# Two-bank feed-forward units that share PSUM tiles with the scores, q and k in one tile, and a new order of steps

## The chip, the cores and the metric

The kernel runs on one core of one Trainium2 chip. Times are device microseconds (us) of that core; lower is better. The five engines that matter here each work through a list of their own in program order: PE (TensorE, matrix products), DVE (VectorE), ACT (ScalarE), POOL (GpSimd) and SP, which issues every DMA. They meet only through semaphores, so an instruction at the head of a list that waits for another engine holds up all that stands behind it on its own.

## The reference

Eight sequences of 448 tokens, twelve heads of 64, model width 768. First an attention with capped scores, then a gated feed-forward layer with a causal convolution of five taps:

```python
scores = cap * np.tanh(q @ k.T / 8 / cap)          # cap = 30
attn   = np.exp(scores - max) / sum                # over the keys
x      = attn @ v                                  # heads side by side: 448 x 768
gate   = sigmoid(sum_i conv_w[i] * shift(x, 4 - i))
out    = (gate * (x @ w_val)) @ w_out
```

w_val, w_out and conv_w come as float64 and are turned into float32 parts by the kernel.

## The kernel before, in words

**Tiling.** Two heads make a pair of 128 rows; there are 48 pairs p, six to a sequence (batch) b. Scores are computed transposed: one `scores(p, i)` (line 317) fills 112 keys by 448 queries for both heads, in two PSUM banks, with the two heads on the two halves of the array's rows. From pair 13 on (NPLAIN) q and k are split into a high and a low float32r part (`half_hi`, `half_lo`, lines 307 and 312), and a score is three products, high-high, high-low, low-high; before that it is one float32 product. ACT then does `tanh` (330) and `exp` (335) in place of two banks each; DVE adds up the exponentials (`add`, 339); PE makes attention times v (`av`, 355) and the sums of exponentials (`sums`, 366), both as float32 products with the two heads on the two halves of the array's columns. DVE turns the sums, takes the reciprocal and multiplies (`turn_sums`, `recip`, `spread`, `mul`: 378 to 404). `x_hi` (ACT) and `x_lo` (DVE) split the result; `conv` makes the gate, its first tap on ACT for p < 11.

**Feed-forward.** For each batch and each of six column blocks d, `val` (438) adds 18 products (six input blocks c, three float32r products each) in one bank; `gate` (DVE, 450) multiplies by the sigmoid; `gated_hi` (ACT) and `gated_lo` (DVE) split that. `out_part` (466) makes one tile of 128 tokens by 384 columns in one bank from 18 products, six or eight tiles a batch; `store` (479) copies it out of PSUM on ACT and `store_out` issues its DMA. `val` and `out_part` are each cut in two halves that are placed separately.

**PSUM.** Eight banks: two score tiles of two banks (`ps_s`), one bank each for `av` and `sums` (`ps_a`), two single banks for the feed-forward (`ps_f`, lent to `av` and `sums` for odd p below 6).

**Order.** The engines' lists are written out by hand. Each step has a time in units of one pair, in the tables at lines 41 to 114 (STEADY, EARLY, TOGETHER, VAL, OUT_EVEN, W_AT and others); `at` collects (time, step), and the steps are emitted in the sorted order with automatic scheduling off for all engines. So a number in a table is a place in every queue that the step uses, SP's included. The three loads of a pair are four DMAs for q, four for k and two for v; a weight block comes in twice, as `w_raw` and, shifted by two bytes, as `w_late`, and is split by `weight_first` (ACT), `weight_second` and `weight_third` (DVE). There is one buffer each of `w_raw` and `w_late`, two of q, k and v.

**Activation sets.** All six sigmoids of a batch stand together at 7.44 (6.92 in the first batch), between pairs' tanh and exp.

Of the kernel before, what the change touches and what calls it, by code (L numbers as in the profile page):

```python
# [35 lines left out]
NX = 7  # L36
NXX = 8
NPT = 6


STEADY = {
    "load_q": -1.9,
    "load_k": -1.85,
    "load_v": -0.6,
    "tq": -0.90,
    "tk": -0.85,
    "scores": (0.0, 0.05, 0.62, 0.67),
    "tanh": (0.06, 0.13, 0.68, 0.75),
    "exp": (0.22, 0.29, 0.82, 0.89),
    "add": (0.52, 1.03, 1.06),  # L50
    "av": (1.10, 1.15, 1.20, 1.25),
    "sums": (1.28,),
    "turn_sums": 1.41,
    "recip": 1.42,
    "spread": 1.44,
    "mul": 1.50,
    "x_hi": 1.52,
    "x_lo": 1.58,
    "conv": (1.60, 1.61, 1.64, 1.67, 1.70),
}  # L60

SPLIT = STEADY | {"q_hi": -0.69, "k_hi": -0.68, "q_lo": -0.475, "k_lo": -0.47}
PAIRED = STEADY | {"add": (0.52, 1.03), "sums": (1.28, 1.29)}
EARLY = {
    "load_q": -1.9,
    "load_k": -1.85,
    "load_v": -0.7,
    "tq": -0.72,
    "tk": -0.70,
    "scores": (-0.50, -0.49, 0.10, 0.11),  # L70
    "tanh": (0.0, 0.01, 0.35, 0.36),
    "exp": (0.17, 0.18, 0.52, 0.53),
    "av": (0.28, 0.37, 0.65, 0.80),
    "sums": (0.29, 0.38, 0.66, 0.81),
    "turn_sums": 1.02,
    "recip": 1.03,
    "spread": 1.04,
    "mul": 1.05,
    "x_hi": 1.30,
    "x_lo": 1.34,  # L80
    "conv": (1.31, 1.50, 1.52, 1.54, 1.56),
}

SIXTH = PAIRED | {k: EARLY[k] for k in ("tq", "tk", "scores", "tanh", "exp")} | {"add": (0.38, 0.62)}


TOGETHER = {
    "scores": (0.0, 0.05, 0.31, 0.32),
    "tanh": (0.06, 0.13, 0.34, 0.36),
    "exp": (0.22, 0.29, 0.47, 0.53),  # L90
    "add": (0.52, 0.60, 0.61),
}
NEXT_TOGETHER = {
    "turn_sums": 1.41, "recip": 1.42, "spread": 1.43, "mul": 1.44, "x_hi": 1.45, "x_lo": 1.54,
    "conv": (1.58, 2.16, 2.17, 2.18, 2.19),
}
PREPARE_TOGETHER = {"q_hi": -0.69, "k_hi": -0.68, "q_lo": -0.44, "k_lo": -0.43}

LATE_X = {"x_lo": 1.76, "conv": (1.78, 1.80, 1.83, 1.86, 1.89)}
NEARLY, NPAIRED, NPLAIN = 6, 11, 13  # L100

VAL_FIRST = (6.50, 6.85, 7.36, 7.74, 8.36, 8.74)
VAL = (6.85, 7.36, 7.74, 8.36, 8.74, 9.36)
SIG_FIRST, SIG_AT = 6.92, 7.44
OUT_EVEN = (9.80, 10.36, 10.74, 11.36, 11.74, 12.36)
OUT_ODD = (9.80, 10.36, 10.74, 10.80, 11.36, 11.74, 11.80, 12.36)
OUT_LATE = (9.80, 10.36, 10.74, 11.74, 12.36, 12.60)
PART = 0.13
KEEP_AT = 10.2
W_AT = (0.70, 1.70, 2.70, 3.70, 4.70, 5.70, 7.1, 8.0, 8.9, 9.7, 10.4, 11.0)  # L110
W_LOAD = -0.5
W_SECOND, W_THIRD, W_THIRD_EARLY = 0.02, 0.05, 0.71
W_FREE = 11.3
CW_LOAD, CW_AT = -0.55, 0.6
EPS = 1e-9
# [13 lines left out]
def float64_split(nc, raw, mid, hi, lo, t):  # L129
# [16 lines left out]
    def third():  # L146
# [7 lines left out]
def load_conv_w(nc, pool, conv_w, cw):  # L154
# [13 lines left out]
    def make():  # L168
        halves = raw.bitcast(U16).rearrange("p n (k h) -> p n k h", h=1)[:, :, 1:3, 0]
        nc.gpsimd.tensor_copy(mid.bitcast(U16).rearrange("p (n k) -> p n k", k=2), halves)  # L170
        for step in float64_split(nc, raw, mid, cwf, lo, t):
            step()
        nc.vector.tensor_tensor(cwf, cwf, lo, op=ALU.add)
# [27 lines left out]
def fast_path(tc, io, u2, q, k, v, w_val, conv_w, w_out, out, capt):  # L201
# [22 lines left out]
    with ExitStack() as ctx:  # L224
        cpool = ctx.enter_context(tc.tile_pool(name="cpool", bufs=1))
        wk = ctx.enter_context(tc.tile_pool(name="wk", bufs=2))
        ps_s = ctx.enter_context(tc.tile_pool(name="ps_s", bufs=2, space=PSUM))
        ps_a = ctx.enter_context(tc.tile_pool(name="ps_a", bufs=1, space=PSUM))
        ps_f = ctx.enter_context(tc.tile_pool(name="ps_f", bufs=2, space=PSUM))
# [4 lines left out]
        def free_scratch():  # L234
            scratch.pop("w").close()
            scratch["qk"] = ctx.enter_context(tc.tile_pool(name="halves", bufs=2))
# [25 lines left out]
        wstate = {}  # L262
# [11 lines left out]
        def late_load(n):  # L274
# [5 lines left out]
            wstate[n] = wstate[n], shifted(late, NH)  # L280

        def weight_first(n):
            _, c, nh, w = wsteps[n]
            t = wsc.tile([P, WC, NH], I32, name="w_t")
            wstate[n] = float64_split(nc, *wstate[n], w[:, c, nh, 0], w[:, c, nh, 1], t)
# [5 lines left out]
        def weight_third(n):  # L291
            wstate.pop(n)[2]()

        state = {}
        loads, vloads = {(name, 0): t[:, PAD:] for name, t in zip("qk", u2)}, {}

        def load(name, src, p):
            if p:
                loads[name, p] = io.tile([P, S], F32, name=name + "n")
                load_blocks(nc, loads[name, p], src, p)  # L300

        def turn(name, p):
            t = wk.tile([P, S], F32, name=name + "t")
            nc.vector.transpose(t, loads.pop((name, p)))
            state.setdefault(p, {})[name] = t

        def half_hi(name, p):
            st = state[p]
            st[name, "h"] = scratch["qk"].tile([P, S], F32R, name=name + "h")
            nc.scalar.copy(st[name, "h"], st[name])  # L310

        def half_lo(name, p):
            st = state[p]
            st[name, "l"] = scratch["qk"].tile([P, S], F32R, name=name + "l")
            less(nc.vector, st[name, "l"], st.pop(name), st[name, "h"])

        def scores(p, i):

            st = state[p]
            ps = ps_s.tile([P, 2, 512], F32, name="pss")  # L320
            c = slice(i * CH, (i + 1) * CH)
            parts = [("k", "q")] if p < NPLAIN else [(("k", x), ("q", y)) for x, y in ("hh", "hl", "lh")]
            for n, (x, y) in enumerate(parts):
                for j, r in enumerate(ROWS):
                    nc.tensor.matmul(  # L325
                        ps[:CH, j, :S], st[x][r, c], st[y][r], start=(n == 0), stop=(n == len(parts) - 1)
# [3 lines left out]
        def tanh(p, i):  # L330
            st = state[p]
            st["p", i] = wk.tile([CH, 2, S], F32, name="pt", bufs=NPT)
# [16 lines left out]
        def bank(p, name):  # L349

            if p < NEARLY and p % 2:
                return ps_f.tile([P, 512], F32, name="psf")
# [13 lines left out]
        def sums(p, i):  # L366

            st = state[p]
            n = len(tables[p]["sums"])
# [5 lines left out]
            if i == n - 1:  # L375
                vloads.pop(p)
# [20 lines left out]
        xs = {}  # L397
        gates = {}

        def norm_mul(p):  # L400
# [3 lines left out]
            gates[p] = wk.tile([P, S], F32, name="gate", bufs=NX), u  # L404

        def x_hi(p):
            xh = wk.tile([P, S], F32R, name="xh", bufs=NXX)
            nc.scalar.copy(xh, gates[p][1][:, PAD:PAD + S])  # L408
            xs[p] = xh

        def x_lo(p):
            xl = wk.tile([P, S], F32R, name="xl", bufs=NXX)
            less(nc.vector, xl, gates[p][1][:, PAD:PAD + S], xs[p])
            xs[p] = xs[p], xl

        def conv(p, i):
            hp = p % NPAIR
            g, u = gates[p]
# [6 lines left out]
            if i == KW - 1:  # L425
                gates[p] = g

        def sigmoid(b, d):
            g = gates[b * NPAIR + d]
# [307 lines left out]
```

## Time and profile before

| | before |
|---|---|
| median of 3 runs | 754.07 us (752.65 to 757.52) |
| profiled execution: span from first to last instruction, the only time given of it | 750.1 us |
| mean granted TensorE clock | 0.996 |
| busy: PE / DVE / ACT / POOL | 724.0 / 591.8 / 533.8 / 7.6 us |
| share of the span: PE / DVE / ACT | 97% / 79% / 71% |
| instructions | 10863 |
| first matmul starts, last matmul starts | 7.70 us, 744.33 us |
| moved by DMA | 63.75 MB |

A row of a group gives the line, the engine, the operation, output and inputs, the shape, the count, the busy time, the mean length of one, and the idle time of the engine just ahead of the group with what ended it. A row of the timeline gives start, length, engine and instruction. The recorded length of a matmul runs on into the next one, so the time that a matmul takes up in a stream is read from the starts of two neighbours.

### The profile page before, as it was taken

What the parts mean: (1) busy time and instruction counts of PE and PEld (TensorE: products, weight loads), DVE (VectorE), ACT (ScalarE), POOL (GpSimd) and SP (SyncE); (2) the same over time, 40 slices, a digit from 0 to 9 for tenths busy, and PEclk for the clock granted to TensorE, in tenths of its full rate; (3) what the DMA queues carried; (4) which work ended last, traced back from release to release, by engine and by line L of the source; (5) the groups of instructions that cost most, each with busy time, mean ns of one, the idle gap of its engine ahead of it and who ended that gap; (6) DMA issues with size and microseconds to landing.
All of it is one profiled execution on the core that took longest, in us unless ns stands there. A gap on an engine that the chain in (4) does not pass through costs nothing.

```text
span 750.1 us, 10863 instructions
## 1 busy us (share of the span) xinstructions
PE 724.0 (97%) x3972; PEld 487.7 (65%) x3972; DVE 591.8 (79%) x972; ACT 533.8 (71%) x708; POOL 7.6 (1%) x16
## 2 busy tenths in 40 slices
PE   5999998999899999999999999999999999999997
PEld 2333654556667777577576866767766776666996
DVE  2799988987987689888898769988898778988410
ACT  4899967777857678686967579487786768775311
POOL 0000000000000000000000000000000000000000
PEclk9999999999999999999999999999999999999999
DMA  6978766753223242234231333223322233200001
GB/s 108 230 191 219 204 168 146 195 131 77 48 38 80 70 84 38 49 71 86 48 67 42 78 81 63 49 63 77 73 38 60 69 79 64 50 24 32 22 21 67
DMA packets 241820, 63.75 MB, mean 85 GB/s; under 512 B 228448, under 2 KB 235616, under 8 KB 241760
## 3 DMA queue, kind: packets, MB, share of 16 engines
q1 hardware_dynamic: 241760, 62.98, 37.4%
q8 instruction: 33, 0.54, 0.3%
q14 instruction: 27, 0.22, 0.1%
HBM read 51.94 MB, written 11.01 MB: 84 GB/s over the span
## 4 chain that ended last, share of the span: by engine, by line
PE 50%; DVE 18%; ACT 16%; issue 3%; SPq 1%; DMA 0%; DVEq 0%; ACTq 0%
PE pss L325 9%; PE psf L474 7%; PE psf L476 7%; PE psf L475 7%; PE psa L362 6%; ACT pt L333 5%; DVE gate L424 5%; PE psf L445 4%; PE psf L446 4%; PE psf L447 4%; ACT pt L337 3%; DVE pa L347 3%; PE psz L374 3%; ACT gate L430 3%; DVE pa L344 2%
## 5 line engine op out<-in xcount | busy, mean ns | idle before, releaser
L333 ACT ACTIVATE pt<-pss,rc 112x896 f32<-112x896 f32 x192 | 185.4, 1006 | 38.9 <-PE pss L325 38.9
L337 ACT ACTIVATE pt<-pt,capt 112x896 f32<-112x896 f32 x192 | 189.7, 1042 | 0.1
L362 PE MATMUL psa<-pt,vn 112*64 112x448 f32 x720 | 146.9, 546 | 0.0
L424 DVE SCALAR_TENSOR_TENSOR gate<-u,cw,gate 128x448 f32<-128x448 f32 x192 | 131.6, 685 | 5.2
L474 PE MATMUL psf<-wo,g_h 128*128 128x384 f32 x336 | 116.6, 347 | 1.2 <-ACT g_h L454 1.2
L476 PE MATMUL psf<-wo,g_l 128*128 128x384 f32 x336 | 113.3, 337 | 0.2
L475 PE MATMUL psf<-wo,g_h 128*128 128x384 f32 x336 | 112.4, 334 | 0.0
L445 PE MATMUL psf<-xh,wv 128*128 128x448 f32 x288 | 107.5, 373 | 2.1 <-DVE gate L451 2.0
L447 PE MATMUL psf<-xl,wv 128*128 128x448 f32 x288 | 104.4, 363 | 0.0
L446 PE MATMUL psf<-xh,wv 128*128 128x448 f32 x288 | 104.3, 362 | 0.0
L362 PEld LDWEIGHTS psa<-pt,vn 112*64 112x64 f32 x720 | 47.4, 136 | 81.1 <-issue 68.1
L347 DVE TENSOR_TENSOR pa<-pt 112x896 f32<-112x896 f32 x84 | 91.0, 1084 | 11.4 <-ACT pt L337 11.4
L474 PEld LDWEIGHTS psf<-wo,g_h 128*128 128x128 f32 x336 | 63.0, 188 | 16.7 <-issue 12.5
L482 ACT COPY osb<-psf 128x384 f32<-128x384 f32 x56 | 26.7, 478 | 61.6 <-PE psf L476 59.9
L454 ACT CAST g_h<-gate 128x448 fp32r<-128x448 f32 x48 | 26.3, 563 | 61.6 <-DVE gate L451 61.5
L382 DVE STREAM_TRANSPOSE zt<-psz 128x448 f32<-128x448 f32 x45 | 28.8, 641 | 52.0 <-PE psz L374 51.9
L445 PEld LDWEIGHTS psf<-xh,wv 128*128 128x128 f32 x288 | 54.0, 187 | 22.1 <-issue 5.4
L476 PEld LDWEIGHTS psf<-wo,g_l 128*128 128x128 f32 x336 | 63.0, 188 | 2.2 <-DVE g_l L239 2.2
L475 PEld LDWEIGHTS psf<-wo,g_h 128*128 128x128 f32 x336 | 63.1, 188 | 0.0
L325 PE MATMUL pss<-qt,kt 64*112 64x448 f32 x208 | 51.2, 610 | 10.0 <-DVE guard L248 7.7
L325 PE MATMUL pss<-qh,kh 64*112 64x448 f32 x280 | 58.5, 412 | 0.0
L408 ACT CAST xh<-u 128x448 fp32r<-128x448 f32 x48 | 27.2, 568 | 42.4 <-DVE u L403 42.2
(74 smaller groups left out, 905.5 us busy)
## 6 DMA issues: line engine op xcount, KB each, us to landing
vn<-in_v_dram SPq DMA_DIRECT2D x96, 112.0 KB, 2.6
out_dram<-osb SPq DMA_DIRECT2D x56, 192.0 KB, 1.9
qn<-in_q_dram SPq DMA_DIRECT2D x188, 56.0 KB, 2.5
kn<-in_k_dram SPq DMA_DIRECT2D x188, 56.0 KB, 2.5
w_raw<-in_moe_w_val_dram SPq DMA_DIRECT2D x12, 384.0 KB, 5.4
w_late<-in_moe_w_val_dram SPq DMA_DIRECT2D x12, 384.0 KB, 4.2
w_raw<-in_moe_w_out_dram SPq DMA_DIRECT2D x12, 384.0 KB, 3.8
w_late<-in_moe_w_out_dram SPq DMA_DIRECT2D x12, 384.0 KB, 4.3
```

The costliest lines, as they stand in the source:

```text
L325: nc.tensor.matmul(ps[:CH, j, :S], st[x][r, c], st[y][r], start=(n == 0), stop=(n == len(parts) - 1))
L333: nc.scalar.activation(st["p", i], st.pop(("s", i)), AF.Tanh, scale=rc8[:CH])
L337: nc.scalar.activation(t, t, AF.Exp, scale=capt[:CH])
L347: nc.vector.tensor_tensor(st["a", i], st["p", 2 * i], st["p", 2 * i + 1], op=ALU.add)
L362: nc.tensor.matmul(st["o"][r, :S], vloads[p][:, j, i], t[:, j], start=(i == 0), stop=(i == NKT - 1))
L424: nc.vector.scalar_tensor_tensor(g, u[:, i:i + S], cw[:, hp, i:i + 1], g, ALU.mult, ALU.add)
L445: nc.tensor.matmul(o, w_h, xh, start=(c == 0), stop=False)
L446: nc.tensor.matmul(o, w_l, xh, start=False, stop=False)
L447: nc.tensor.matmul(o, w_h, xl, start=False, stop=(c == NCC - 1))
L474: nc.tensor.matmul(o, g_h[:, d, s], w_h, start=(d == 0), stop=False)
L475: nc.tensor.matmul(o, g_h[:, d, s], w_l, start=False, stop=False)
L476: nc.tensor.matmul(o, g_l[:, d, s], w_h, start=False, stop=(d == NCC - 1))
```

## The change

1. `ps_f` is gone. `ps_s` has three tiles of two banks, and scores, `val`, `out_tile` and (odd p below 6) `av` with `sums` take them in turn.
2. `val(b, e)` does two column blocks at once, 36 products in a two-bank tile; `out_tile(b, t)` does 128 tokens by all 768 columns, 36 products. Neither is cut into halves. The number and kind of products is the same.
3. `gate`, `sigmoid`, `gated_hi`, `gated_lo` and `store` work on 896 (store: 768) columns at once, so there are half as many of them. `osb` has one buffer of double size, and a store is one DMA of double size.
4. q and k stand in one tile: `turn`, `half_hi` and `half_lo` are one instruction instead of two (pair 0 keeps two transposes).
5. The tables are replaced by PAIR, BATCH and WEIGHTS, one number for every step and every one of 29 columns (pairs 0 to 14, a cycle of 12 pairs, the last two); `load_v`, weight loads and stores have new places too. In the repeating part the four scores of a pair stand together, ahead of a `val` or `out_tile` or behind one, and sigmoids stand at two places (even batches) or three (odd ones).
6. The space of the weights' scratch tiles, free once the weights are split, gives more buffers late in the run (`late`): the high part of q and k, one more of `gate` and of `x`, two more of `pt`.

```diff
-        ps_s = ctx.enter_context(tc.tile_pool(name="ps_s", bufs=2, space=PSUM))
+        ps_s = ctx.enter_context(tc.tile_pool(name="ps_s", bufs=3, space=PSUM))
         ps_a = ctx.enter_context(tc.tile_pool(name="ps_a", bufs=1, space=PSUM))
-        ps_f = ctx.enter_context(tc.tile_pool(name="ps_f", bufs=2, space=PSUM))
+
+        def banks():
+            return ps_s.tile([P, 2, 512], F32, name="pss")
...
+        def turn(p):
+            t = wk.tile([P, 2, S], F32, name="qkt")
+            if p:
+                nc.vector.transpose(t.rearrange("p j s -> p (j s)"), loads.pop(p).rearrange("p j s -> p (j s)"))
...
+        def half_hi(p):
+            st = state[p]
+            st["h"] = scratch["late"].tile([P, 2, S], F32R, name="qkh")
+            nc.scalar.copy(st["h"], st["l"])
...
+        def sigmoid(b, e):
+            g = pairs[b * NPAIR // 2 + e]
             nc.scalar.activation(g, g, AF.Sigmoid)
...
+        def val(b, e):
+            psums[b, e] = o = banks()
+            for c in range(NCC):
                 xh, xl = xs[b * NPAIR + c]
-                w_h, w_l = (wv[:, c, d // NPH, x, cols] for x in range(2))
-                nc.tensor.matmul(o, w_h, xh, start=(c == 0), stop=False)
-                nc.tensor.matmul(o, w_l, xh, start=False, stop=False)
-                nc.tensor.matmul(o, w_h, xl, start=False, stop=(c == NCC - 1))
+                for j in range(2):
+                    d = 2 * e + j
+                    cols = slice(d % NPH * P, (d % NPH + 1) * P)
+                    w_h, w_l = (wv[:, c, d // NPH, x, cols] for x in range(2))
+                    nc.tensor.matmul(o[:, j, :S], w_h, xh, start=(c == 0), stop=False)
+                    nc.tensor.matmul(o[:, j, :S], w_l, xh, start=False, stop=False)
+                    nc.tensor.matmul(o[:, j, :S], w_h, xl, start=False, stop=(c == NCC - 1))
...
+        def out_tile(b, t):
+            t0 = TL * (1 - b % 2) + t * P
+            s = slice(t0, t0 + P)
+            psums[b, "o", t] = o = banks()
             g_h, g_l = gated["h"], gated["l"]
+            for d in range(NCC):
+                for nh in range(2):
+                    w_h, w_l = (wo[:, d, nh, x] for x in range(2))
+                    nc.tensor.matmul(o[:, nh, :NH], g_h[:, d, s], w_h, start=(d == 0), stop=False)
...
+        def store(b, t):
             row = b * S - TL * (b % 2) + t * P
+            osb = wk.tile([P, 2, NH], F32, name="osb", bufs=1)
+            nc.scalar.copy(osb, psums.pop((b, "o", t))[:, :, :NH])
```

Of the tables, the rows that the prediction speaks of (the columns are batch 0, batch 1, the even ones, the odd ones and the last):

```diff
+BATCH = {
+    "sigmoid": (
+        (6.8378, 7.1151, 7.3249, 5.4748, 6.5827),
+        (7.0106, 8.7084, 6.8322, 8.4311, 7.4049),
+        (7.6515, 9.8857, 7.5925, 9.522, 9.3631),
+    ),
+    "val": (
+        (6.992, 7.5079, 7.2616, 7.6082, 7.6597),
+        (7.6034, 8.623, 8.4304, 8.6508, 7.68),
+        (8.8352, 9.6391, 9.3585, 9.6306, 9.4801),
+    ),
...
+    "out_tile": (
+        (11.3777, 10.6175, 10.1157, 10.6972, 10.6774),
+        (11.9328, 11.3228, 11.1432, 11.3339, 11.5725),
+        (12.5653, 12.1816, 12.3996, 12.1317, 11.8472),
+        (None, 13.1921, None, 13.0834, 12.6071),
+    ),
...
+WEIGHTS = {
+    "weight_load": (-4.3624, .9119, 2.3733, 3.1736, 4.1326, 4.9596, 6.5272, 7.0111, 8.1881, 9.2169, 9.598, 10.6669),
```

In the lists that the new tables give, the steps at the start come in these orders. SP: v of pair 0, `w_raw` 0, q of pair 1, k of pair 1, `w_late` 0, q and k of pair 2, conv_w, v of pair 1. PE: scores 0 and 1 of pair 0, its scores 3, `av` 0, its scores 2, then scores 0 of pair 1. In the repeating part (batch 3): val(3,2), two scores of pair 28, three `av` and the `sums` of pair 27, its last `av`, two scores of pair 28, out_tile(3,0).

More of the change, by code (lines that the diff above doesn't have):

```diff
@@ L34 @@
 WC = 2
-NX = 7
 NXX = 8
 NPT = 6
[L41 to L59, printed above, removed]
-}
@@ L62 @@
[L62 to L81, printed above, removed]
-}
@@ L84 @@
[L84 to L91, printed above, removed]
-}
[L93 to L97, printed above, removed]
@@ L170, in make @@
         nc.gpsimd.tensor_copy(mid.bitcast(U16).rearrange("p (n k) -> p n k", k=2), halves)
-        for step in float64_split(nc, raw, mid, cwf, lo, t):
-            step()
+        first, second, third = float64_split(nc, raw, cwf, lo, t)
+        first()
+        second()
+        third(mid)
         nc.vector.tensor_tensor(cwf, cwf, lo, op=ALU.add)
@@ L368, in sums @@
             st = state[p]
-            n = len(tables[p]["sums"])
+            n = sum(row[column(p)] is not None for row in PAIR["sums"])
             if i == 0:
@@ L395, in spread, with gate_of @@
             nc.vector.transpose(st["zt"].rearrange("p (c e) -> p c e", e=BLK), rc)
-        xs = {}
-        gates = {}
+        xs, us, pairs = {}, {}, {}
+        def gate_of(p):
+            e = p // 2
+            if e not in pairs:
+                late = p >= NLATE and e % (NG + 1) == NLATE // 2 % (NG + 1)
+                pairs[e] = (scratch["late"] if late else wk).tile([P, 2, S], F32, name="gate", bufs=1 if late else NG)
+            return pairs[e][:, p % 2]
         def norm_mul(p):
@@ L459, in keep_tail, with gate, gated_hi, gated_lo @@
+        def gate(b, e):
+            g = pairs[b * NPAIR // 2 + e]
+            nc.vector.tensor_tensor(g, psums.pop((b, e))[:, :, :S], g, op=ALU.mult)
+        def gated_hi(b, e):
+            nc.scalar.copy(gated["h"][:, 2 * e:2 * e + 2, TL:], pairs[b * NPAIR // 2 + e])
+        def gated_lo(b, e):
+            r = slice(2 * e, 2 * e + 2)
+            less(nc.vector, gated["l"][:, r, TL:], pairs.pop(b * NPAIR // 2 + e), gated["h"][:, r, TL:])
         def keep_tail():
@@ new lines, in fast_path @@
+        steps = dict(
+            sigmoid=sigmoid, val=val, gate=gate, gated_hi=gated_hi, gated_lo=gated_lo, out_tile=out_tile, store=store, store_out=store_out,
+        )
+        for name, f in steps.items():
+            for i, row in enumerate(BATCH[name]):
+                for b in range(B):
+                    if row[batch_column(b)] is not None:
+                        at(NPAIR * b + row[batch_column(b)], f, b, i)
+        for b in range(0, B, 2):
+            at(NPAIR * b + BATCH["keep_tail"][0][batch_column(b)], keep_tail)
```

395 lines of the change are left out of this document (253 added, 142 removed).

## The prediction

> **What bounds the kernel now.** I read the page's busy shares, then the windows over one repeating stretch, then the timeline for what a matmul takes up, and last the rows in which PE waits.
>
> ```profile
> span 750.1 us, 10863 instructions
> ...
> PE 724.0 (97%) x3972; PEld 487.7 (65%) x3972; DVE 591.8 (79%) x972; ACT 533.8 (71%) x708; POOL 7.6 (1%) x16
> ```
>
> PE is the bound, but its recorded matmuls overlap, so 97% does not say how much could go. The repeating unit is two batches, 12 pairs. From the sigmoids of batch 2 (277.29 us) to those of batch 4 (452.28):
>
> ```profile
> 277.29:361.48 84.19, 83.60 (x482) 58.02 (x481) 74.16 (x121) 64.31 (x86) 1.73 (x2) 1.00 0.32 64
> 361.48:452.28 90.80, 90.15 (x518) 64.36 (x517) 73.79 (x121) 65.28 (x88) 0.00 (x0) 1.00 0.31 64
> 277.29:452.28 174.99, 173.75 (x998) 122.39 (x997) 147.95 (x241) 129.59 (x174) 1.73 (x2) 1.00 0.31 64
> ```
>
> (Columns: length, then busy of PE, weight loads, DVE, ACT, POOL, clock, DMA share.) The clock is full. How much of 174.99 is products, seen from the starts:
>
> ```profile
> 238.29 0.33 PE L474 MATMUL psf<-wo,g_h 128*128 128x384 f32 x1
> ...
> 238.81 0.33 PE L474 MATMUL psf<-wo,g_h 128*128 128x384 f32 x1
> ...
> 240.19 0.34 PE L476 MATMUL psf<-wo,g_l 128*128 128x384 f32 x1
> 240.46 0.46 PE L325 MATMUL pss<-qh,kh 64*112 64x448 f32 x2
> 240.76 0.37 PE L325 MATMUL pss<-ql,kh 64*112 64x448 f32 x2
> 240.96 0.36 PE L325 MATMUL pss<-qh,kl 64*112 64x448 f32 x2
> 241.16 0.36 PE L325 MATMUL pss<-qh,kh 64*112 64x448 f32 x2
> ...
> 241.56 0.37 PE L325 MATMUL pss<-qh,kl 64*112 64x448 f32 x2
> 241.86 1.35 PE L362 MATMUL psa<-pt,vn 112*64 112x448 f32 x6
> ```
>
> ```profile
> 158.88 1.69 PE pss L325 x8
> ...
> 241.93 3.16 PE psa L362 x16
> ```
>
> ```profile
> 186.10 0.36 PE L445 MATMUL psf<-xh,wv 128*128 128x448 f32 x1
> ...
> 186.70 0.36 PE L445 MATMUL psf<-xh,wv 128*128 128x448 f32 x1
> ...
> 188.50 0.38 PE L325 MATMUL pss<-qh,kl 64*112 64x448 f32 x2
> ...
> 190.87 0.47 PE L445 MATMUL psf<-xh,wv 128*128 128x448 f32 x1 [1.99 <-DVE gate L451]
> ...
> 191.18 0.36 PE L446 MATMUL psf<-xh,wv 128*128 128x448 f32 x1
> 191.38 0.37 PE L447 MATMUL psf<-xl,wv 128*128 128x448 f32 x1
> ```
>
> Three output products take 0.52 us (238.29 to 238.81), three value products 0.60, two score products side by side 0.20, four `av` steps 3.16 in the chain (and two float32 score steps, before pair 13, 1.69). By the code, 12 pairs hold 216 value products (43.2 us), 252 output products (43.7), 48 score steps of three (28.8), 48 `av` and 12 `sums` steps of 0.79 (47.4): 163.1 us. The other 11.9 are two things.
>
> First, **switches** between products that fill the array and products on half of it. 240.19 to 240.46 is 0.27 where 0.17 is usual; the first score product of a burst holds the next up for 0.30 instead of 0.20, and so does the last (241.56 to 241.86); the first full product after a burst takes 0.31 (190.87 to 191.18) instead of 0.20. So a burst of scores costs 0.2 beyond its products and a change from or to full ones 0.1 each. The lists hold, per 12 pairs, 24 bursts (4.8 us) and 15 changes from full and 16 to full (3.1). Second, a rest of 4.0 us: waits, and the end of `av` runs.
>
> **The change, part by part.** *Steady stretch.* The products stay. The new lists, sorted from the tables, have 13 bursts of scores, 12 changes from and 12 to full: 2.6 + 2.4 us, 2.9 less per 12 pairs. (Four scores in one burst instead of two, and units of 36 products instead of 9.) The rest of 4.0: its largest repeated part is the turn from the last `val` to the first output. Before, two scores and 15 output products stand ahead of the first that needs the last block, 1.2 + 2.6 = 3.8 us of cover for the chain below; in the new list for batch 3, four scores, four `av` and one `sums` (6.4 us) and then the first four of six input blocks of the tile (24 products, 4.2 us) stand ahead of them, 10.6 us. These rows price the chain and the merged operations:
>
> ```profile
> L333 ACT ACTIVATE pt<-pss,rc 112x896 f32<-112x896 f32 x192 | 185.4, 1006 | 38.9 <-PE pss L325 38.9
> L337 ACT ACTIVATE pt<-pt,capt 112x896 f32<-112x896 f32 x192 | 189.7, 1042 | 0.1
> L347 DVE TENSOR_TENSOR pa<-pt 112x896 f32<-112x896 f32 x84 | 91.0, 1084 | 11.4 <-ACT pt L337 11.4
> L451 DVE TENSOR_TENSOR gate<-psf,gate 128x448 f32<-128x448 f32 x48 | 29.0, 617 | 11.9 <-PE psf L447 11.9
> L482 ACT COPY osb<-psf 128x384 f32<-128x384 f32 x56 | 26.7, 478 | 61.6 <-PE psf L476 59.9
> L430 ACT ACTIVATE gate<-gate 128x448 f32<-128x448 f32 x48 | 23.3, 565 | 0.1
> L430 ACT ACT_TABLE_LOAD x8 | 10.3, 1283 | 0.1
> L337 ACT ACT_TABLE_LOAD x7 | 9.0, 1283 | 0.1
> ```
>
> Merged, `gate`, `gated_hi` and `gated_lo` take 1.08, 1.04 and 1.08 us (by the 896-column rows), 3.2 in sequence, well under 10.6 with some 5 us queued on DVE between them. I therefore let half of the rest go, 2.0 (bounds 0 and 4.0). Steady: 2.9 + 2.0 = 4.9 us per 12 pairs; pairs 13 to 47 are 2.92 such units: **-14.3 us** (-8.5 to -20).
>
> *DVE and ACT* are not the bound: 147.95 and 129.59 of 174.99. A merge saves 2 x 617 - 1084 = 0.15 us on DVE; per 12 pairs there are 12 `turn`, 12 `half_lo`, 6 `gate`, 6 `gated_lo`: 5.4 less. On ACT a merge saves 2 x 565 - 1042 = 0.09: 12 `half_hi`, 6 sigmoids, 6 `gated_hi`, 7 stores, about 2.8 less. But the sigmoids of a batch no longer stand together. In the trace a load of 1.28 us stands before the first sigmoid of a batch and one before the first exp after it (8 and 7 in all). In the new order an exp stands between them, so batches have 2, 3, 2, 3, 2, 3, 2 and 1 visits, 18 instead of 8: 20 loads more, 25.7 us in all, three visits or 7.7 us per 12 pairs. ACT goes to 134.5 and DVE to 142.6, both under the 170 that PE then needs, so PE's work hides it, as long as the loads stand where no score tile waits for its tanh. The Trainium skill, page "ScalarE: Activation LUTs", section "Table sets: the hidden batching unit", says to group calls by table set, which speaks against this change; its section "What ACT_TABLE_LOAD costs" adds a drain of 1.38 us to each, and by that estimate 20 loads would cost ACT 53 us. The trace's rows show 0.1 us of idle time before all the loads together, so the sum goes by 1.28.
>
> *Start.* The issues of q and k for pair 1 stand behind v of pair 0 and a weight block now:
>
> ```profile
> 6.27 1.88 SPq L185 DMA_DIRECT2D qn<-in_q_dram  x4
> 8.19 2.04 SPq L185 DMA_DIRECT2D kn<-in_k_dram  x4
> 10.27 1.01 SPq L197 DMA_DIRECT2D vn<-in_v_dram  x2
> ...
> 12.26 0.65 DVE L304 STREAM_TRANSPOSE kt<-kn 128x448 f32<-128x448 f32 x1 [1.36 <-DMA kn<-in_k_dram]
> ...
> 14.22 1.02 SPq L271 DMA_DIRECT2D w_raw<-in_moe_w_val_dram  x2
> ```
>
> k of pair 1 is issued by 12.3 instead of 10.2 and lands, behind 0.8 MB of weights, two to three us later than the 12.26 of before; the merged transpose waits for both. In PE's new list only four scores and one `av` (4 x 0.85 + 0.79) stand ahead of the first score of pair 1, so it idles about 2.5 us: **+2.5** (0 to +5).
>
> *Pairs 1 to 12.* Here ACT is the bound:
>
> ```profile
> 45.00:60.00 15.00, 14.67 (x74) 4.88 (x72) 14.49 (x27) 14.96 (x19) 0.00 (x0) 1.00 0.81 223
> 60.00:75.00 15.00, 14.23 (x71) 4.89 (x68) 14.01 (x24) 14.72 (x19) 0.00 (x0) 1.00 0.89 197
> ```
>
> Its work is the same but for one more visit to the sigmoids (2.6 us); full and half products change 12 times instead of 23 (-1.1). **+1** together. DMA is 0.81 to 0.89 busy and weight blocks stand nearer to their use than before, so the bounds are -5 and +12.
>
> *Tail.* The last store is 768 columns: about 0.3 us more copy (478 ns for 384) and twice the bytes in one DMA: **+1** (0.3 to 2.2). The three loads, stores and the keeping of the tail on POOL (1.73 of 175 us) are otherwise moved under PE's work; SP issues half as many stores.
>
> Sum: -14.3 + 2.5 + 1 + 1 = -9.8: span 740.3. The median of the runs stands 3.97 above the profiled span (754.07 to 750.1), so about 744; I take **742**, since the waits outside the steady stretch (two follow) have no term of their own:
>
> ```profile
> 124.86 0.99 PE L374 MATMUL psz<-pa,ones 112*64 112x448 f32 x4 [2.34 <-DVE pa L347]
> ```
>
> This one and the 1.99 before 190.87 are places where a step came too close behind its input; the new lists keep neither of the two neighbourhoods.
>
> **Rivals.** *All waits go.* If steady waits vanish (-20) and pairs 1 to 12 gain 5, the span is 750.1 - 20 + 2.5 - 5 + 1 = 728.6, time 732. For: the new lists place every step on its own. Against: they leave less room around the loads.
>
> *The early part eats it.* The single buffers of `w_raw` and `w_late` make each block wait for the split of the last:
>
> ```profile
> w_raw<-in_moe_w_val_dram SPq DMA_DIRECT2D x12, 384.0 KB, 5.4
> ```
>
> A load takes 1.0 us to issue (14.22) and 5.4 to land, and in the new list a block's first step comes 3 to 10 us of ACT's work (median 7, summed from the rows above) after the second step of the one before; in the old list it is 6 to 14 (median 9). If ten of the eleven later blocks are late by one us, ACT, the early bound, ends 10 later: 752.
>
> *Slower: ACT's loads come between PE and its tiles.* With three shared tiles, a score step needs the tile of three units ago, so the third and fourth score behind a `val` or `out_tile` wait for `gate`, `store` or the first tanh. A visit to the sigmoids (2.57 of loads and 1.04) in ACT's queue just there holds PE up for the whole of it. If all ten added visits are exposed so, +25.7: 742 + 25.7 = 768. It decides from about five of them on (13 us, more than the gain). For: the 1.99 us row shows such a wait for a tile. Against: the load stands before the exp, not before the tanh, and a tanh needs none after a sigmoid in this trace. By the Trainium skill's drain of 1.38 us ("ScalarE: Activation LUTs", "What ACT_TABLE_LOAD costs") ten visits would cost 28 more; no row here shows one.
>
> *It does nothing:* the freed switches turn up again as waits, 752 to 756.
>
> **How the numbers follow.** Forecast 742 (own range 734 to 750): 0.45. All waits go: 0.17. Early part: 0.18. ACT's loads: 0.12. Nothing: 0.08. The range takes in the first three and part of the fourth: 728 to 759. About 1% can be told from no change: under 746.5 faster, over 761.6 slower. Faster: 0.45 x 0.8 + 0.17 + some of the early cases 0.09 = 0.62. Slower 0.12. Same 0.26.
>
> **What would show it.** After: 12 pairs in the middle last about 170 us instead of 175; 18 and 17 loads of 1283 ns; DVE rows of 1.08 us for `gate`, ACT busy near 548, DVE near 572; the first score of pair 1 waits for its transpose; PE's rows keep 0.17 and 0.20 spacing. I am wrong if the stream of full products slows when two banks alternate, if tanh rows show long idle before scores with sigmoids just ahead, or if the first 150 us grow by over 6.

## The result, and the profile after

The kernel after takes **733.29 us** (median of 4 runs, 732.06 to 733.99), beside 753.36 us (751.69 to 757.52) for the kernel before on the same chip: a ratio of 0.9737, with an interval of 0.970 to 0.9775. Forecast were 742 us, with a range of 728 to 759. The profiled execution of after took 733.66 us, its span is 731.8, so the spans differ by 18.3 us; the medians differ by 20.1. Every run on record takes 1.7 to 2.1 us more than its own span, so the profiled execution of before (span 750.1) took some 752 us, less than the median of its runs. From the page of after:

```profile
span 731.8 us, 10598 instructions
...
PE 707.7 (97%) x3972; PEld 489.8 (67%) x3972; DVE 563.2 (77%) x842; ACT 554.9 (76%) x617; POOL 5.9 (1%) x16
```

PE's share is 97% again, although 18 us went: a share cannot show this change. Two batches of the middle can. The windows of after, from the first value product of batch 2 (267.85 us) over batch 3 (349.41) to batch 4 (columns as in the prediction):

```profile
267.85:349.41 81.56, 81.56 (x482) 58.10 (x481) 65.38 (x95) 65.29 (x73) 1.19 (x2) 1.00 0.33 68
349.41:437.50 88.09, 88.09 (x518) 64.63 (x517) 75.36 (x111) 71.11 (x78) 0.00 (x0) 1.00 0.32 64
267.85:437.50 169.65, 169.65 (x997) 122.73 (x997) 140.74 (x205) 136.40 (x150) 1.19 (x2) 1.00 0.32 66
```

12 pairs take 169.65 us, 5.3 less than the 174.99 of before, and PE's records now cover every moment. The same stretches of 12 pairs, summed from start to start of PE's matmuls in the two traces:

| us per 12 pairs, start to start | before | after |
|---|---|---|
| inside runs of output products | 44.85 | 43.32 |
| inside runs of `av` and `sums` | 42.91 | 41.28 |
| inside runs of value products | 42.12 | 42.57 |
| scores, and every change of kind | 45.13 | 42.46 |

The last two lines are the switches and give 2.2 together; the first two give 3.2, which is for the most part waits. In before the waits are the first output tile of a batch (gaps of 0.53, 0.28 and 0.38 us instead of 0.17, at 312.5 and again at 396.8) and `sums` behind an `add`; in after no gap of that kind is left.

Where along the run did the 18.3 us go? Call progress the sum of what the products done so far take at the lengths of the prediction (683.4 us for the whole), and lag the start of a product less the progress:

| lag in us at a progress of | 0 | 5 | 50 | 100 | 180 | 680 | then, to the end of the span |
|---|---|---|---|---|---|---|---|
| before | 7.7 | 9.8 | 13.7 | 17.2 | 28.0 | 60.9 | 5.8 |
| after | 7.7 | 12.3 | 18.6 | 20.9 | 24.2 | 42.2 | 6.2 |

Up to 100 (pair 8 or so) after falls 3.7 behind; from 100 to 180 (to about pair 14) it gains 7.4; from there to the end 15.0; the tail costs 0.4. The first of these figures is that of one trace and moves by some 2 us: the run with more bursts, below, has the lists of after up to pair 14, but its granted clock is 0.57 from 18 to 20 us and 0.58 from 20 to 22, where after has 1.00, and its lag at 100 is 22.8.

The groups of after that answer to those shown of before:

```profile
L453 DVE STREAM_TRANSPOSE qkt<-qkn 128x896 f32<-128x896 f32 x47 | 51.8, 1102 | 15.9 <-DMA qkn<-in_k_dram 10.6 <-DMA cw_raw<-in_moe_conv_w_dram 4.8 <-DMA vn<-in_v_dram 0.3
L613 DVE TENSOR_TENSOR gate<-pss,gate 128x896 f32<-128x896 f32 x24 | 26.2, 1090 | 39.1 <-PE pss L609 38.7 <-ACT gate L595 0.4
L595 ACT ACT_TABLE_LOAD x18 | 23.1, 1283 | 0.2
L643 ACT COPY osb<-pss 128x768 f32<-128x768 f32 x28 | 22.4, 798 | 75.0 <-PE pss L638 75.0
L493 ACT ACT_TABLE_LOAD x17 | 21.8, 1283 | 0.3
```

There are 18 and 17 loads, and merged rows of 1.1 us. The start has the wait that was forecast; the timeline of PE:

```profile
13.14 1.01 PE L478 MATMUL pss<-qkt 64*112 64x448 f32 x4
16.85 2.51 PE L478 MATMUL pss<-qkt 64*112 64x448 f32 x12 [2.70 <-DVE qkt L453]
```

What the prediction did not look at is ACT's waits up to 150 us. They were, in before (in all, times, longest):

```profile
ACT xh L408 <- DVE u L403: 12.6, 6, 4.0
ACT g_h L454 <- DVE gate L451: 4.8, 3, 3.5
```

and in after:

```profile
ACT w_t L282 <- DMA w_raw<-in_moe_w_val_dram: 6.1, 3, 3.1
ACT pt L489 <- PE pss L478: 4.9, 3, 3.6
```

The windows between 100 and 150 us, before first and after second, show what that made of the pairs in which the weights are split and the feed-forward already runs:

```profile
100.00:150.00 50.00, 46.70 (x223) 25.48 (x224) 44.11 (x72) 37.06 (x47) 1.70 (x2) 0.97 0.64 161
```

```profile
100.00:150.00 50.00, 48.88 (x243) 25.80 (x242) 47.28 (x70) 46.51 (x55) 1.02 (x2) 1.00 0.79 189
```

In before no engine is full there: PE, DVE and ACT wait for one another. In after DVE works almost without a gap. PE's longest waits of before between 80 and 200 us, in all, times, longest:

```profile
PE psz L374 <- DVE pa L347: 4.2, 3, 2.3
PE psf L445 <- DVE gate L451: 2.0, 1, 2.0
```

Three of these four lie between a progress of 100 and 180: 2.34 us at 122, 1.09 at 153 and 1.99 at 189 us, 5.4 together, where after has one of 1.1. The wait at 122 is also followed by a lowered clock (0.50 from 126 to 128 us, see the last section), by an estimate 1.7 us more (half of the 3.41 us for which the clock's record shows it). That makes 6.0 of the 7.4.

### The profile page after: what moved, and what is told of

Its sections match the earlier page's. It is cut to its first block, busy times and chain, and to the rows that moved or that the text cites. A ratio compares the mean times of both kernels' runs of the same rounds, so it can differ in the third digit from the quotient of the medians.

```text
span 731.8 us, 10598 instructions
## 1 busy us (share of the span) xinstructions
PE 707.7 (97%) x3972; PEld 489.8 (67%) x3972; DVE 563.2 (77%) x842; ACT 554.9 (76%) x617; POOL 5.9 (1%) x16
## 4 chain that ended last, share of the span: by engine, by line
PE 76%; ACT 3%; DVE 2%; issue 1%; DVEq 0%; ACTq 0%
PE psa L522 16%; PE pss L478 13%; PE pss L636 8%; PE pss L638 8%; PE pss L637 8%; PE pss L607 7%; PE pss L609 7%; PE pss L608 7%; PE psz L534 4%; ACT pt L493 1%; ACT pt L489 0%; ACT L493 0%; DVE gate L591 0%; ACT pl L489 0%; ACT qkh L462 0%
## 5 line engine op out<-in xcount | busy, mean ns | idle before, releaser
L636 PE MATMUL pss<-wo,g_h 128*128 128x384 f32 x336 | 114.9, 342 | 0.0
L638 PE MATMUL pss<-wo,g_l 128*128 128x384 f32 x336 | 112.5, 335 | 0.0
L637 PE MATMUL pss<-wo,g_h 128*128 128x384 f32 x336 | 112.4, 334 | 0.0
L607 PE MATMUL pss<-xh,wv 128*128 128x448 f32 x288 | 106.2, 369 | 0.6 <-ACT pt L489 0.6
L609 PE MATMUL pss<-xl,wv 128*128 128x448 f32 x288 | 104.5, 363 | 0.0
L608 PE MATMUL pss<-xh,wv 128*128 128x448 f32 x288 | 104.1, 362 | 0.0
L636 PEld LDWEIGHTS pss<-wo,g_h 128*128 128x128 f32 x336 | 63.0, 188 | 15.7 <-issue 8.0
L607 PEld LDWEIGHTS pss<-xh,wv 128*128 128x128 f32 x288 | 54.0, 188 | 16.5 <-ACT pt L489 9.0
L453 DVE STREAM_TRANSPOSE qkt<-qkn 128x896 f32<-128x896 f32 x47 | 51.8, 1102 | 15.9 <-DMA qkn<-in_k_dram 10.6
L638 PEld LDWEIGHTS pss<-wo,g_l 128*128 128x128 f32 x336 | 63.1, 188 | 0.1
L637 PEld LDWEIGHTS pss<-wo,g_h 128*128 128x128 f32 x336 | 63.1, 188 | 0.0
L478 PE MATMUL pss<-qkh 64*112 64x448 f32 x280 | 58.3, 412 | 0.0
L609 PEld LDWEIGHTS pss<-xl,wv 128*128 128x128 f32 x288 | 54.0, 188 | 3.8
L608 PEld LDWEIGHTS pss<-xh,wv 128*128 128x128 f32 x288 | 54.0, 187 | 3.4
```

What stands on the lines that cost most here:

```text
L478: nc.tensor.matmul(ps[:CH, j, :S], st[x][r, 1, c], st[y][r, 0], start=(n == 0), stop=(n == len(parts) - 1))
L607: nc.tensor.matmul(o[:, j, :S], w_h, xh, start=(c == 0), stop=False)
L608: nc.tensor.matmul(o[:, j, :S], w_l, xh, start=False, stop=False)
L609: nc.tensor.matmul(o[:, j, :S], w_h, xl, start=False, stop=(c == NCC - 1))
L636: nc.tensor.matmul(o[:, nh, :NH], g_h[:, d, s], w_h, start=(d == 0), stop=False)
L637: nc.tensor.matmul(o[:, nh, :NH], g_h[:, d, s], w_l, start=False, stop=False)
```

## The experiments

**The price of a switch: more bursts, same products.**

```diff
-            for _, _, f, a in sorted(events, key=lambda e: e[:2]):
+            for f, a in interleave([e[2:] for e in sorted(events, key=lambda e: e[:2])]):
                 f(*a)
```

(`interleave` moves the next `av` or `sums` whose inputs stand earlier in the list between two scores of a burst, from pair 14 on.)

> The kernel after, with one thing changed: from pair 14 on, the av and sums steps that stand behind a burst of four scores on PE are put between its scores, so that 38 bursts of scores become 98. All products and all other lists are the same. Theory (switches cost): each of the 60 new bursts takes 0.2 us by the rows of the kernel before, and the av run that it cuts about 0.1 more, so the time is 12 to 18 us longer than that of the kernel after (733.3): 745 to 751 us. Rival (only waits count, and the new order has slack for such details): within 2 us of 733.3.

Measured: 763.68 us, ratio to before 1.0139 [1.0115, 1.0163]; 30.4 us over the kernel after. Four scores and three `av` of after, and one turn of the new pattern (up to the start of the next score), in PE's timeline:

```profile
275.15 0.46 PE L478 MATMUL pss<-qkh 64*112 64x448 f32 x2
...
277.92 2.48 PE L522 MATMUL psa<-pt,vn 112*64 112x448 f32 x12
280.22 0.92 PE L534 MATMUL psz<-pa,ones 112*64 112x448 f32 x4
```

```profile
283.49 0.45 PE L478 MATMUL pss<-qkh 64*112 64x448 f32 x2
...
284.28 0.97 PE L522 MATMUL psa<-pt,vn 112*64 112x448 f32 x4
285.19 0.46 PE L478 MATMUL pss<-qkh 64*112 64x448 f32 x2
```

In the burst a score takes (277.92 - 275.15) / 4 = 0.69 and an `av` (280.22 - 277.92) / 3 = 0.77, together 1.46; one by one they take 1.70. So an added burst costs 0.24 us, near the 0.3 that was priced, and 60 of them 14 us. Of the other 16 us some 12 are new waits: PE's waits over 12 pairs of this run (273.39 to 453.98 us) sum to 4.0 us, where after has none, and pairs 13 to 47 are 2.92 such units. A likely reason, not shown, is that attention now ends later. Some 2 us more lie ahead of pair 14, in the halved clock near 20 us of this trace, and have nothing to do with the bursts. The two longest groups of waits:

```profile
PE psz L534 <- DVE pa L500: 1.7, 2, 0.9
PE psa L522 <- DVE u L567: 1.3, 1, 1.3
```

Switches cost about what the rows of before said. The rival, that slack absorbs them, falls. The slack in the new order is also small: moving only PE's list cost nearly as much in waits as in switches.

**No table loads.**

```diff
-            nc.scalar.activation(g, g, AF.Sigmoid)
+            nc.scalar.activation(g, g, AF.Tanh)
```

> The kernel after with tanh in the place of the sigmoid, so the gate is another function and the output is not the reference's. All table loads but the first go, 34 of 1.28 us or 44 us of ACT; nothing else changes. Theory (the loads are hidden behind PE): within 3 us of 733.3. Rival (loads stand between PE and its shared tiles): up to 10 us or more shorter, 723 or less, by waits of scores for their tiles that go.

The kernel then leaves out the sigmoid. Measured: 733.51 us, ratio 0.9734 [0.9706, 0.9761], 0.2 us from after. The page:

```profile
PE 710.2 (97%) x3972; PEld 490.5 (67%) x3972; DVE 562.9 (77%) x842; ACT 508.3 (69%) x582; POOL 6.1 (1%) x16
```

ACT loses 46.6 us of work and the time does not move: the loads are hidden, all of them.

**Two instructions instead of each merged one.**

```diff
-            nc.vector.tensor_tensor(g, psums.pop((b, e))[:, :, :S], g, op=ALU.mult)
+            o = psums.pop((b, e))
+            for j in range(2):
+                nc.vector.tensor_tensor(g[:, j], o[:, j, :S], g[:, j], op=ALU.mult)
```

(and so in `sigmoid`, `gated_hi`, `gated_lo`, `turn`, `half_hi`, `half_lo`, `store`)

> The kernel after with sigmoid, gate, gated_hi, gated_lo, turn, half_hi, half_lo and the copy of store as two instructions of one half each again; order, tiles and products are the same. By the rows this gives DVE 0.15 and ACT 0.09 us more for each split step. Theory (the gain is the order and the three shared tiles): 733 to 736 us. Rival (the merged instructions make the chains short enough): 740 us or more, with waits of PE for gate and for the halves of q and k.

Measured: 732.69 us, ratio 0.9743 [0.9718, 0.9768]: the same as after, with 241 more instructions on DVE and ACT.

```profile
PE 707.2 (97%) x3972; PEld 490.0 (67%) x3972; DVE 571.6 (78%) x972; ACT 562.8 (77%) x728; POOL 6.1 (1%) x16
```

The merged instructions save 8 us each on DVE and ACT and nothing of the time that can be told from the spread of the runs. The gain is in the rest of the change: order, tiles and the added buffers (part 6), of which no run takes out the buffers alone.

**The load of pair 1 ahead of the weights.**

```diff
     "load_q": (
-        (-12.3822, -4.978, -4.432,
+        (-12.3822, -5.55, -4.432,
     "load_k": (
-        (-2.4596, -4.3386, -3.8142,
+        (-2.4596, -5.5, -3.8142,
```

> The kernel after with the eight DMA issues of q and k of pair 1 ahead of those of the first weight block on SP's list; nothing else is changed. q and k then start 1.0 us earlier and share the first bytes with no weights. Theory of the prediction (the wait of 3.2 us before the first score of pair 1 adds to the span): 2 to 2.5 us shorter than 733.3. Rival (ACT is the bound from there on, and is busy without a gap from 11.6 to 20.7 us): the wait on PE gets shorter, the time stays within 0.5 us.

Measured: 733.67 us, ratio 0.9747 [0.9726, 0.9767]. PE's timeline:

```profile
14.75 2.60 PE L478 MATMUL pss<-qkt 64*112 64x448 f32 x12 [0.43 <-DVE qkt L453]
...
39.61 2.37 PE L522 MATMUL psa<-pt,vn 112*64 112x448 f32 x4 [2.68 <-DMA vn<-in_v_dram]
```

The first score of pair 1 is 2.1 us earlier, and all of it is given back by 40 us, where the product that waits for v of a later pair starts no earlier (38.60 in after, 39.61 here). The wait of 2.68 us there is followed by a halved clock (0.50 from 40 to 42 us, 1.00 in after), yet the lag at a progress of 50 is 18.6 in both. So the wait at the start adds nothing to the span of after; something later sets the pace. The wait is not free in every execution: in the run with more bursts the halved clock near 20 us stands right behind this wait, and its 2 us are still there at pair 14.

**Room for ACT in the first 70 us.** (weight blocks 2 and 4, conv_w, v of pairs 2 and 4)

```diff
     "load_v": (
-        (-4.6334, -.187, .1176, -.1034, -.0121,
+        (-4.6334, -.187, -.55, -.1034, -.27,
-    "weight_first": (-1.1328, 1.6924, 2.7279, 3.3553, 4.6625,
-    "weight_second": (-.9859, 2.0484, 2.7298, 3.9326, 4.6781,
-    "weight_third": (-.1634, 2.2924, 3.2326, 3.9671, 4.7948,
+    "weight_first": (-1.1328, 1.6924, 2.91, 3.3553, 4.83,
+    "weight_second": (-.9859, 2.0484, 2.92, 3.9326, 4.84,
+    "weight_third": (-.1634, 2.2924, 3.2326, 3.9671, 4.85,
-W_FREE, CW_LOAD, CW_AT = 12.0218, .6042, .9935
+W_FREE, CW_LOAD, CW_AT = 12.0218, .6042, 1.5
```

> The kernel after with only early places changed: the first and second step of weight blocks 2 and 4 stand two or three tanh later on ACT and DVE (where ACT waited 2.3 and 3.1 us for the block's DMA), conv_w's steps two exps later (1.3 us), and v of pairs 2 and 4 is issued earlier. Theory (ACT is the bound of the first 70 us, so what it idles there adds to the span): 3 to 6 us shorter than the kernel after, 727.5 to 730.5. Rival (as with the earlier load of pair 1, the next wait takes its place): 732 to 734.

Measured: 733.15 us, ratio 0.9741 [0.9723, 0.9759]: no change. ACT's waits at blocks 2 and 4 go, and one of 2.97 us comes at block 3, where after has 0.69. The row puts it down to a transpose on DVE that was just done, but the block's load ends there too: issued at 45.08 us, it lands up to 7.6 us later.

```profile
53.11 0.92 ACT L282 ACTIVATE w_t<-w_raw 128x768 f32<-128x768 f32 x1 [2.97 <-DVE zt L553]
```

The DMA queue from 44 to 54 us (packets, MB, share of 16 engines) is full:

```profile
q1 hardware_dynamic: 3371, 2.45, 95.8%
```

At a progress of 50 the lag is 16.6 here and 18.6 in after, but by 70 it is 20.4 here and 19.8 in after. So ACT's idle time does not set the pace of this stretch either. That the DMA engines do is what the full queue points to; no run took bytes away to show it.

**Pairs 6 to 13 of the kernel before: four runs.** First the splits of the weights behind the adds:

```diff
-            at(t0 + W_SECOND, weight_second, n)
-            at(third[n], weight_third, n)
+            later = 0.15 if t0 > NEARLY else 0
+            at(t0 + W_SECOND + later, weight_second, n)
+            at(third[n] + later, weight_third, n)
```

> The kernel before with the second and third step of weight blocks 6 to 11 put 0.15 of a pair later in DVE's list, behind the adds of that pair, and the loads that follow them moved by as much; nothing of the change is in it. In the kernel before, DVE waits there for ACT's first step with an add queued behind, and PE waits 1.3, 2.9 and 1.6 us for that add at 105, 122 and 153 us. Theory (these waits are a matter of place and add to the span): 3 to 6 us shorter than the kernel before of the same job. Rival (they only stand in for other waits of the same stretch): within 1.5 us of it.

Measured: 754.34 us, ratio 1.0019 [1.0003, 1.0035]. The three waits for adds go, but the splits now stand ahead of the product u on DVE, ACT stands at x_hi for it, and PE's scores wait for the tanh behind that (ACT, then PE, of this run):

```profile
129.80 0.57 ACT L408 CAST xh<-u 128x448 fp32r<-128x448 f32 x1 [4.41 <-DVE u L403]
...
131.89 1.84 PE L325 MATMUL pss<-qt,kt 64*112 64x448 f32 x4 [3.51 <-ACT pt L333]
```

Behind this wait the clock is at 0.50 from 131.9 to 138.7 us.

Then x_hi, x_lo and conv behind the next tanh:

```diff
+        for p in range(NEARLY, NPLAIN):
+            tables[p] = tables[p] | {"x_hi": 1.755, "x_lo": 1.76, "conv": (1.757, 1.80, 1.83, 1.86, 1.89)}
```

> The kernel before with x_hi, x_lo and conv of pairs 6 to 12 put behind the next pair's second tanh in the lists of ACT and DVE; nothing of the change is in it. In the kernel before, ACT waits between 90 and 160 us with x_hi at the head of its list for the product u, 1.9, 3.9, 4.0 and 3.8 us, with tanh and the weights' first step queued behind. Theory (this chain of ACT, DVE and PE makes the slack that the new order took away, 7.4 us between 100 and 180 us): 4 to 7 us shorter than the kernel before of the same job. Rival (ACT has room there, and PE's waits have another source): within 1.5 us of it.

Measured: 748.25 us, ratio 0.9939 [0.9915, 0.9963], 4.8 us shorter than before. At a progress of 180 its lag is 24.7 instead of 28.0. The waits at 153 and 189 us are gone, 3.1 us. Left are two waits of PE for adds, the second of them that at 122 us of before, again with the halved clock behind it:

```profile
106.56 0.97 PE L374 MATMUL psz<-pa,ones 112*64 112x448 f32 x4 [1.21 <-DVE pa L347]
124.74 0.97 PE L374 MATMUL psz<-pa,ones 112*64 112x448 f32 x4 [2.31 <-DVE pa L347]
```

Both moves together:

> The kernel before with both moves of the two runs before: the late steps of weight blocks 6 to 11 behind the adds, and x_hi, x_lo and conv of pairs 6 to 12 behind the next tanh. With the splits later alone, DVE reached the product u later and ACT stood at x_hi for it, 4.4 us at 125 us, so PE's scores waited 3.5 us; that wait has no place any more when x_hi stands behind the tanh. Theory (a circle of ACT, DVE and PE, in which the wait goes only if both orders are mended): 743 to 746.5 us, below the 748.2 of the one move alone. Rival (the second move takes all that there is): 747 to 750.

Measured: 751.64 us, ratio 0.998 [0.9966, 0.9994]. These two waits shrink to 0.5 and 0.2, and one of 1.6 comes at 141 us. The blocks' loads, which follow the splits through the single buffer, come later and hold up ACT, by 2.5, 2.0 and 2.7 us; PE waits 2.5 us for a tanh behind the first of these:

```profile
129.96 0.90 ACT L139 ACTIVATE w_t<-w_raw 128x768 f32<-128x768 f32 x1 [2.51 <-DMA w_raw<-in_moe_w_out_dram]
```

Last, x_hi later and the adds earlier, with the splits and loads where they were:

```diff
+        for p in range(NEARLY, NPLAIN):
+            tables[p] = tables[p] | {"add": (0.38, 0.62) if p == NEARLY else (0.52, 0.91) if p < NPAIRED else (0.52, 0.91, 0.92), "x_hi": 1.755, ...}
```

> The kernel before with x_hi, x_lo and conv of pairs 6 to 12 behind the next tanh, as in the run of that move alone, and the last adds of pairs 7 to 12 ahead of the splits of the weights in DVE's list instead of behind them; no split and no load is moved. In the run of the first move alone, sums still waited 1.7 and 2.8 us for adds that stood behind splits, at 105 and 122 us. In the run in which the splits were moved, those two waits went, but the loads of the blocks came later too and ACT waited 2.5, 2.0 and 2.7 us for them, which gave it all back. Theory (these waits are a matter of place, and the loads were what spoilt that run): 743.5 to 746.5 us, 2 to 4 below the 748.2 of the first move alone. Rival (the adds only stand in for another wait): 747 to 749.

Measured: 750.06 us, ratio 0.9969 [0.9952, 0.9987]. Adds and splits now both stand ahead of `gate`, which ACT waits for with a tanh queued behind (DVE, ACT, PE of this run):

```profile
120.88 1.09 DVE L347 TENSOR_TENSOR pa<-pt 112x896 f32<-112x896 f32 x1
...
125.33 0.62 DVE L451 TENSOR_TENSOR gate<-psf,gate 128x448 f32<-128x448 f32 x1
...
125.98 0.56 ACT L454 CAST g_h<-gate 128x448 fp32r<-128x448 f32 x1 [4.22 <-DVE gate L451]
...
127.50 3.33 PE L325 MATMUL pss<-qt,kt 64*112 64x448 f32 x8 [4.52 <-ACT pt L333]
```

The theory that these waits can be taken out one by one held for x_hi and fell for the adds. What stands: the slack of this stretch of before is a circle through ACT, DVE and PE. One move takes out 4.8 us by the medians (3.3 by the lags of the two traces); each of the three runs that put adds ahead of splits passed the wait on to another step. The new order, in which every step has another place, takes out 7.4 by the lags.

**Which part lets the scores stand together?** Four scores in one burst, in the kernel before:

```diff
+        for p in range(NPLAIN + 1, NP):
+            tables[p] = tables[p] | {"scores": (0.0, 0.05, 0.06, 0.07)}
```

> The kernel before with the four scores of a pair in one burst from pair 14 on, ahead of av, still on two score tiles; nothing else of the change is in it. That is the grouping without the third tile: 68 bursts become 34, by the rows 34 times 0.2 us or 7 us less. Theory (grouping needs the third tile): the third and the fourth score each wait for a tanh of 1.0 us, at least 1.1 us for each of 34 pairs, so 30 us or more longer than the kernel before. Rival (ACT is early enough): 5 to 7 us shorter.

Measured: 838.19 us, ratio 1.1142 [1.1104, 1.118]. From 200 us on, the time inside runs of scores goes from 75.4 to 138.2 us. Waits between 280 and 700 us, the weight load of the score among them:

```profile
PEld pss L325 <- ACT pt L333: 50.3, 56, 2.7
...
PE pss L325 <- ACT pt L333: 29.0, 33, 2.3
```

With the third tile, shared by scores and the feed-forward, added to that:

```diff
-        ps_s = ctx.enter_context(tc.tile_pool(name="ps_s", bufs=2, space=PSUM))
+        ps_s = ctx.enter_context(tc.tile_pool(name="ps_s", bufs=3, space=PSUM))
...
+        class ps_f:
+            tile = staticmethod(lambda shape, dt, name: ps_s.tile([P, 2, 512], F32, name="pss")[:, 0])
```

> The kernel before with two parts of the change: three tiles of two banks that scores and the feed-forward share (a product of the feed-forward still fills one bank of its tile), and the four scores of a pair in one burst from pair 14 on. The tables are else as before, nothing is merged. With two score tiles that burst cost 85 us. Theory (the third tile is what lets the scores stand together): most of the 85 us goes, and the time is within 12 us of the kernel before, 741 to 765. Rival (the new places of all other steps are needed for it): 20 us or more above the kernel before, since the fourth score waits for the tanh of the first and the next unit for the second.

Measured: 829.27 us, ratio 1.1015 [1.098, 1.105]. Scores wait less (105.5 us inside their runs), but value products now wait for the tile that a tanh still reads:

```profile
PEld pss L447 <- ACT pt L335: 27.4, 9, 4.9
...
PE pss L447 <- ACT pt L335: 20.7, 5, 4.1
```

Some 17 us of the loss do not come from the bursts, though: this run shares the tiles from its first pair on, and its lag at a progress of 100, before any burst, is already 33.9, where before has 17.2. From 180 to 680 the lag grows by 94 us here, by 116 in the run with two tiles and by 33 in before. In that stretch the third tile takes back 22 of the 83 us.

And the first output tile later, in the kernel before:

```diff
-OUT_EVEN = (9.80, 10.36, 10.74, 11.36, 11.74, 12.36)
-OUT_ODD = (9.80, 10.36, 10.74, 10.80, 11.36, 11.74, 11.80, 12.36)
-OUT_LATE = (9.80, 10.36, 10.74, 11.74, 12.36, 12.60)
+OUT_EVEN = (10.29, 10.36, 10.74, 11.36, 11.74, 12.36)
+OUT_ODD = (10.29, 10.36, 10.74, 10.80, 11.36, 11.74, 11.80, 12.36)
+OUT_LATE = (10.29, 10.36, 10.74, 11.74, 12.36, 12.60)
```

> The kernel before with the first output tile of each batch put behind the attention products and sums of the next pair, ahead of its last two scores. In the kernel before it waits about 0.8 us in each second batch for the last gated blocks. Theory (with two score tiles the output tile is also what covers the tanh between two bursts of scores): the wait for gated goes, but the next scores wait for a tile of which the tanh has only begun, so the time is the same or up to 10 us longer. Rival (the turn's wait is a matter of place alone): 3 to 4 us shorter.

Measured: 784.42 us, ratio 1.0411 [1.0385, 1.0437], 32 us longer where 0 to 10 were expected. Output products lose their waits (from 200 us on 159.3 to 154.6 us inside their runs), and the scores, with no output tile to cover the tanh, lose more (75.4 to 106.5):

```profile
PE pss L325 <- ACT pt L333: 19.6, 5, 3.9
```

Part of that is a lowered clock behind the waits (mean granted clock 0.969, in before 0.996; see the last section).

So neither the grouping, nor the third tile with grouping, nor a later output tile is a gain by itself: each leaves a tanh, a gate or a store uncovered. The steady gain belongs to tiles and places together, as far as these runs go. Not tried are the new order on separate tiles for scores and feed-forward, and the new order without the added buffers of part 6; what each of these does alone is open.

## Why the prediction was right, and where it was wrong

- **Steady stretch.** Forecast 4.9 us per 12 pairs and 14.3 in all; measured 5.3 and 15.0. The two terms hold as well: switches 2.9 forecast, 2.2 measured (scores, changes and value products), with 0.24 us per burst in the run with more bursts; waits 2.0 forecast (half of 4.0), 3.2 measured. The half was a choice, and more than half went: that the sum came so near is in part luck.
- **DVE and ACT hidden.** Right: without any of the 35 loads the time is the same, and with the instructions unmerged too. ACT came to 554.9 us (548 forecast): the merges save 7.9 there, by the run without them, instead of some 11, which is half of the difference. DVE came to 563.2 (572 forecast), although the merges save 8.4 there instead of some 20. The rest of both is not explained. The Trainium skill, page "ScalarE: Activation LUTs", section "What ACT_TABLE_LOAD costs", adds a drain of 1.38 us to a load; here 0.2 and 0.3 us of idle time stand before all 18 and 17 loads, so this trace does not agree.
- **Start, +2.5.** The wait was there (2.70 us), but not its price: the run that took 2.1 us of it away is no shorter. It was counted as a term of its own although the next stretch takes it up.
- **Pairs 1 to 12, +1.** This term failed. With the start it was forecast at +3.5. Up to pair 8 the trace gives +3.7, with waits for v and for weight blocks (6.1 us on ACT), but over the whole stretch it gives -3.7 (3.7 less 7.4). The term took ACT for the bound of all these pairs from two windows between 45 and 75 us; between 100 and 150 us ACT works 37.06 of 50.
- **The waits outside the steady stretch, -2.** The same failure from the other side: two single waits of PE were given 2 us off the final sum, without a term, and the stretch from about pair 9 to 14, where both stand, gained 7.4. The page's rows showed PE's end of the circle only. The window with PE at 46.70, DVE at 44.11 and ACT at 37.06 of 50 us, and 12.6 us of ACT waiting at the head of its list for u, were there to be read.
- **Tail, +1.** +0.4, within its bounds.
- **From the span to the median, +3.97.** The forecast set the median of before's runs against the span of another, faster run. Each run takes only 1.7 to 2.1 us more than its own span, and the median of after stands 1.5 above the profiled span. So about 2.5 of the 8.7 us by which 742 is too high come from here, and most of the rest from the two stretches before the steady one.
- **Rivals.** "All waits go" gave 732 and is nearest, but by other amounts: 20 and 5 us in the steady and early parts, where 15.0 and 3.7 were measured (7.4 less 3.7). "The early part eats it" saw ACT wait for weight blocks, which happened (three times, 6.1 us), but cost at most 3.7 us that the next stretch gave back twice. "ACT's loads" is excluded by the run without them. "It does nothing" is excluded by the result.

What stays open: which of the new places make up the 7.4 us, of which no run recovered more than 4.8; what the added buffers do; and what paces the first 100 us of after, where two runs that removed waits gained nothing. None of these runs is faster than the kernel after by more than the spread of its runs.

## What to carry to other kernels

Price switches between kinds of matmuls from the starts of neighbours, and count them in the lists before and after: that term held within a microsecond per 12 pairs. Where a window shows no engine full, look at what stands at the head of each list, on all engines, not only on the bound; a wait there can be part of a circle, and moving one step passed it on in three of four runs here. A wait that a profile shows is not a price until the work behind it is known to have nothing else to wait for; and a price that is read in one stretch, as ACT's bound was here, does not hold for the next one until its window has been read too.

## What was not expected of the hardware

A wait of PE can cost more than its length. After PE's wait of 4.52 us in the last run of the four, the windows show the granted clock (third column from the end):

```profile
122.00:126.00 4.00, 0.99 (x6) 0.20 (x4) 3.82 (x6) 0.02 (x1) 0.00 (x0) 1.00 0.38 105
126.00:128.00 2.00, 0.49 (x2) 0.45 (x4) 1.42 (x3) 2.00 (x3) 1.37 (x2) 0.87 1.00 304
128.00:130.00 2.00, 2.00 (x8) 0.60 (x4) 1.90 (x5) 2.00 (x3) 0.05 (x1) 0.50 1.07 310
```

The clock is 0.50, and the eight score matmuls take 3.33 us, where eight take 1.76 later in the same run (at 134.14 us). Over all traces of this case, after the first 20 us: gaps between two starts of 1.3 to 2.2 us are followed by a mean clock below 0.97 in the next 3 us in 6 of 75 cases; of 2.2 to 2.6 us in 6 of 13; of 2.6 to 3 us in 9 of 10; of 3 to 3.5 us in 3 of 6; of over 3.5 us in all 16. Each time that the clock is lowered before the end of the work, its records show 0.50 for 3.41 us or twice that. The kernel before has one such place (its wait at 122 us), the kernel after none. In the three longest runs it is a part of the loss, in the last of them most of it: the clock is at 0.50 for 47 us in all with four scores in a burst, 59 with the third tile and 51 with the later output tile, and 9 in before itself. If PE worked throughout these, that is by an estimate (half of the difference) 19 of 85, 25 of 77 and 21 of 32 us. The Trainium skill, page "TensorE: Matmul & The Clock Gate", section "Part 1: The HAM clock gate", names an idle window of about 3.4 us; the halved clock agrees, but here gaps from 2.35 us on, the matmul at their head included, were enough in some cases.
